# Attention ahead of two MoE layers: the softmax reciprocals take another way, and the attention stage is put in a new order

## The chip, the cores and the metric

The kernel runs on one core of a Trainium2 chip. The metric is the device time of one execution in microseconds (us); times of several runs are given as a median with the lowest and the highest. The engines are TensorE (PE), VectorE (DVE), ScalarE (ACT), GpSimd (POOL) and SyncE (SP), whose queue issues all transfers of this kernel.

## The reference, cut to what matters

```python
scores = scale * np.matmul(q, k.transpose(0, 1, 3, 2))      # 4 batches, 8 heads, 576 tokens, 64 wide
thresh = np.max(scores, axis=-1, keepdims=True) - tau
scores = np.where(scores >= thresh, scores, -1000000000.0)
attn = np.exp(scores - np.max(scores, axis=-1, keepdims=True))
attn = attn / (np.sum(attn, axis=-1, keepdims=True) + 1e-09)
x = np.matmul(attn, v)                                      # put together as 2304 tokens x 512
h = x @ w_in;  x = (h * np.tanh(softplus(h))) @ w_out       # first MoE layer, d_ff 2048
g = x @ w_gate
out = (silu(g) * (x @ w_val)) @ w_out2                      # second layer, d_ff 1536
```

The change touches the division by the row sum, which is done as a multiplication of the attention output by the reciprocal, and the order of the work around it.

## The kernel before, in words

**Stages.** `attention()` works off 16 pairs of heads; `moes()` follows with two layers, each a list of blocks (a group of hidden units times a third `r` of the tokens), computed by a scheme with seven products per block that take seven prepared pieces of the input (B11, T1, B22, T2, T3, B21, T4). The pieces of the first block, r = 0, are prepared during attention (function `beside` in `kern`, class `Pieces`: `turn` subtracts, `split` makes a high and a low half, `store` writes 768 KB to DRAM) and fetched into `xp` tiles at the start of `moes()`. Weights arrive as `raw` tiles and are converted by ACT, DVE and POOL (`Weights.convert`).

**One pair p.** SP loads q, k and v; ACT and POOL split q and k into high and low halves; SP copies them into the tile `stk` (`stack`, L240). For i = 0 to 8 (four row blocks of two heads, and one of both heads' tails): `scores` on PE (L95 or L104), `rowmax` on DVE (L112), `thresh` on POOL (L116), `expo` on ACT (L122), `mask` on DVE (L130, which also sums the rows into `su`). `trans` on PE turns the masked block in 128x128 steps (L157) into a PSUM bank `g`, and `evac` on ACT copies it to `pt`. When half of the row blocks are there (u = 0, then u = 1), `av` on PE multiplies by v (L180, 20 matmuls). Banks: `s` has 3 buffers, `g` has 2, which `av` and the transposes share.

**The reciprocals.** For each u: `added` on POOL adds 1e-9 (L185), `recip` on DVE (L190), `rwide` on POOL repeats each reciprocal over 64 columns (L197; for u = 1 also L199), `rbc` on PE turns the result, so that it lies along the token axis, into a `g` bank (L205; for u = 1 also L207 with the constant `own`), `rcopy` on ACT copies it to `rs` (L213), and `xout` on DVE multiplies the `av` bank by `rs` into the result x (L219).

**What sets the order.** Each step is entered in a `Plan` with an engine, a cost, the steps it waits for, the buffers it takes and frees, and a rank from the table `RANK` plus `PERIOD` times the pair (ranks with 0, 1 and z are for pairs 0, 1 and 15). `Plan.order` simulates the engines with these costs and emits the steps in the order found; each engine then works its queue strictly in that order. The plan of `attention()` is emitted as a whole ahead of that of `moes()`, SP's transfers included. In `moes()` the first `raw` loads have the lowest rank, then come the fetches of `xp`.

Of the kernel before, what the change touches and what calls it, by code (L numbers as in the profile page):

```python
# [23 lines left out]
def consts(tc, cp, tau):  # L24
    nc = tc.nc
    idf = cp.tile([P, P], F32, name="idf")
    make_identity(nc, idf)
    t = cp.tile([P, 3], F32, name="tau")
    nc.sync.dma_start(out=t[:, 0:1], in_=tau.partition_broadcast(P))

    nc.vector.tensor_scalar(out=t[:, 1:2], in0=t[:, 0:1], scalar1=0.0, scalar2=-1.0, op0=ALU.max, op1=ALU.mult)
    nc.vector.tensor_scalar(out=t[:, 2:3], in0=t[:, 0:1], scalar1=0.0, scalar2=0.125, op0=ALU.is_ge, op1=ALU.mult)

    own = cp.tile([P, P], F32, name="own")
    fold = cp.tile([P, 64], F32, name="fold")
    nc.vector.memset(own, 0.0)
    for h in range(2):
        a = slice(64 * h, 64 * h + 64)
        nc.vector.tensor_copy(out=fold[a, :], in_=idf[a, a])
        nc.vector.memset(own[a, a], 1.0)  # L40
    return dict(idf=idf, own=own, fold=fold, ntau=t[:, 1:2], cs=t[:, 2:3])


def attention(tc, cst, q, k, v, x, beside, S=576):
# [12 lines left out]
    idf, own, fold, ntau, cs = (cst[x] for x in ("idf", "own", "fold", "ntau", "cs"))  # L57
# [7 lines left out]
    qt = [pl.tile([P, 2, P], F32R, name=f"qt{i}") for i in range(2)]  # L65
    for t in qt:
        nc.vector.memset(f(t), 0.0)


# [62 lines left out]
    def bank(nm):  # L132
# [39 lines left out]
    def av(p, u, j0, j1):  # L172

        d = st[p]
        if j0 == 0:
            d["av", u] = bank(f"av{p}_{u}")
# [5 lines left out]
    def added(p, u):  # L182
        d = st[p]
        a = slice(4 * u, 4 + 5 * u)
        nc.gpsimd.tensor_scalar(out=d["su"][:, a], in0=d["su"][:, a], scalar1=1e-9, scalar2=0.0, op0=ALU.add, op1=ALU.add)  # L185

    def recip(p, u):
        d = st[p]
        a = slice(4 * u, 4 + 5 * u)
        nc.vector.reciprocal(out=d["r"][:, a], in_=d["su"][:, a])  # L190

    def rwide(p, u):

        d = st[p]
        w = d["rw", u] = pw.tile([P, 320], F32, tag="rw", name=f"rw{p}_{u}", bufs=SLOTS["rw"])
        r = d["r"][:, 4 * u:4 * u + 4].rearrange("p (c h) -> p c h", h=2)[:, :, :, None].to_broadcast([P, 2, 2, 64])
        nc.gpsimd.tensor_scalar(out=w[:, 0:256].rearrange("p (c h d) -> p c h d", c=2, h=2), in0=r, scalar1=1.0, scalar2=1.0, op0=ALU.mult, op1=ALU.mult)  # L197
        if u:
            nc.gpsimd.tensor_scalar(out=w[:, 256:320], in0=fold, scalar1=d["r"][:, 8:9], scalar2=1.0, op0=ALU.mult, op1=ALU.mult)  # L199

    def rbc(p, u):
        d = st[p]
        g = d["rg", u] = bank(f"rg{p}_{u}")
        for c in range(2):
            nc.tensor.transpose(g[:, 128 * c:128 * c + 128], d["rw", u][:, 128 * c:128 * c + 128], idf)  # L205
        if u:
            nc.tensor.matmul(out=g[:, 256:320], lhsT=own, rhs=d["rw", u][:, 256:320], start=True, stop=True)  # L207

    def rcopy(p, u):
        d = st[p]  # L210
        d["rs", u] = pw.tile([P, 320], F32, tag="rs", name=f"rs{p}_{u}", bufs=SLOTS["rs"])
        n = 256 + 64 * u
        nc.scalar.copy(out=d["rs", u][:, 0:n], in_=d["rg", u][:, 0:n])  # L213

    def xout(p, u):
        d = st[p]
        n = 256 + 64 * u
        for to, c0, c1 in xslices(p, 256 * u, n):
            nc.vector.tensor_tensor(out=to, in0=d["av", u][:, c0:c1], in1=d["rs", u][:, c0:c1], op=ALU.mult)  # L219
# [49 lines left out]
    turns = []  # L269
    for p in range(NP + 2):  # L270
        for i in range(16):
            turns.append((p, "T", i))
            turns += [(p - a // 16, "A", u) for u, a in enumerate(AFTER) if i == a % 16]
    turns = {x: ("g", n) for n, x in enumerate(x for x in turns if 0 <= x[0] < NP)}
    plan = Plan(SLOTS, WAIT)
    for p in range(NP):
        ranks = {x: iter(y) for x, y in RANK.items()}
        small = iter(range(16))

        def op(eng, cost, fn, *a, key, after=(), take=(), free=()):  # L280
            kind = (key[0] if eng != "DMA" else "D" + key[0] if key[1] == "load" else "st") + OWN.get(p, "")
            plan.op(eng, cost, lambda p=p: fn(p, *a), (p, *key), [(p, *x) for x in after], take, free, PERIOD * p + next(ranks[kind]))

        for nm in "qk":
            op("DMA", 1.2, load, nm, key=(nm, "load"), take=["n"])
            if nm == "q":
                op(*(("Pool", 1.0, inputs, "q", "scale", nc.gpsimd) if p else ("DVE", .4, inputs, "q", "scale", nc.vector)), key=("q", "scale"), after=[("q", "load")])
            if nm == "q" and p == 0:
                op("Pool", 1.5, zeros, key=("q", "zeros"), take=["stk"])
                for h in range(2):  # L290
                    op("ACT", .573, firstparts, "hi", h, key=("q", "hi", h), after=[("q", "scale"), ("q", "zeros")])
                    op("DVE", .7, firstparts, "lo", h, key=("q", "lo", h), after=[("q", "hi", h)], free=["n"] * h)
                continue
            op("ACT", .573 + .053 * (nm == "k"), inputs, nm, "hi", key=(nm, "hi"), after=[("q", "scale") if nm == "q" else ("k", "load")], take=[nm])
            op(*(("Pool", 1.4 + .15 * (nm == "k"), inputs, nm, "lo", nc.gpsimd) if p else ("DVE", .75, inputs, nm, "lo", nc.vector)), key=(nm, "lo"), after=[(nm, "hi")], free=["n"])
        op("Pool", .8, tails, key=("t",), after=[("q", "stack", 1) if p else ("q", "lo", 1)], take=["qt"], free=["q"] * (p > 0))
        op("DMA", 1.3, load, "v", key=("v", "load"), take=[vslot(p)])
        for nm, cost in (("q", 1.3), ("k", 2.6)) * (p > 0):
            for h in range(2):
                op("DMA", cost, stack, nm, h, key=(nm, "stack", h), after=[(nm, "lo"), ("q", "stack", 0)][:2 if (nm, h) != ("q", 0) else 1], take=["stk"] * ((nm, h) == ("q", 0)))  # L300
        for i in range(9):
            c, h = divmod(i, 2)
            made = [(y, "stack", z) for y in "qk" for z in ([h] if i < 8 else [0, 1])] if p else [("q", "lo", h if i < 8 else 1), ("k", "lo")]
            op("PE", .53 if p and i < 8 else .81, scores, i, key=("S", i), after=made + [("t",)] * (i == 8), take=["s"], free=["k", "qt", "stk"] if i == 8 else [])
            op("DVE", .68, rowmax, i, key=("R", i), after=[("S", i)] + [("R", 0)] * (i > 0), take=["sm"] * (i == 0))
            op("Pool", .26, thresh, i, key=("H", i), after=[("R", i)])
            op("ACT", .7, expo, i, key=("E", i), after=[("R", i)], take=["e"])
            op("DVE", .8, mask, i, key=("M", i), after=[("E", i), ("H", i)] + [("M", i - 1)] * h, take=["pp"] if h == 0 else [], free=["s", "e"])
            for m0, n in (((0, 3),), ((3, 3), (6, 3)))[h] if i < 8 else ((0, 4), (4, 2)):
                g = turns[p, "T", next(small)]  # L310
                op("PE", .11 * n, trans, c, m0, n, key=("T", c, m0), after=[("M", i)], take=[g] + ["pt"] * (m0 == 0 and c in (0, 2)), free=["pp"] * (m0 == (6 if c < 4 else 4)))
                op("ACT", .365 if c < 4 else .54 if m0 == 0 else .21, evac, c, m0, n, key=("V", c, m0), after=[("T", c, m0)], free=[g])
            if i in (3, 8):
                u = int(i == 8)
                op("Pool", .26, added, u, key=("P", u), after=[("M", 3)] if u == 0 else [("M", 7), ("M", 8)])
                op("DVE", .2, recip, u, key=("Q", u), after=[("P", u)])
                op("Pool", .38 + .2 * u, rwide, u, key=("rw", u), after=[("Q", u)], take=["rw"], free=["sm"] * u)
                g = turns[p, "T", next(small)]
                op("PE", .22 + .22 * u, rbc, u, key=("B", u), after=[("rw", u)], take=[g], free=["rw"])
                op("ACT", .31, rcopy, u, key=("C", u), after=[("B", u)], take=["rs"], free=[g])  # L320
                ready = [("V", y, z) for y in ((0, 1), (2, 3))[u] for z in (0, 3, 6)] + [("V", 4, 0), ("V", 4, 4)] * u + [("v", "load")]
                for n, (j0, j1) in enumerate(PARTS):
                    end = j1 == 5
                    op("PE", (.432, .538)[u] * (j1 - j0), av, u, j0, j1, key=("A", u, n), after=ready, take=[] if n else [turns[p, "A", u]], free=(["pt"] + [vslot(p)] * u) * end)
                    ready = [("A", u, n)]
                op("DVE", .335 + .067 * u, xout, u, key=("x", u), after=[("C", u)] + ready, free=[turns[p, "A", u], "rs"])
# [8 lines left out]
class Plan:  # L335
# [14 lines left out]

    def __init__(self, slots, wait):
# [11 lines left out]
    def op(self, eng, cost, fn, key, after, take, free, rank):  # L363
        o = dict(eng=eng, cost=cost, fn=fn, key=key, after=after, take=[], free=[], rank=rank, n=len(self.ops), loose=self.loose)
# [8 lines left out]
    def order(self, ops, strict):  # L373
# [24 lines left out]
        n, turn = 0, False  # L398
        while True:
            best = None  # L400
            for e in engines:
                found = []
                if queue[e] and not queue[e][-1]["left"]:
                    o = queue[e][-1]
                    found.append((max(clock[e], o["t"]), -1e9, n, o))
# [697 lines left out]
```

## Time and profile before

| | us |
|---|---|
| median of 3 runs (lowest, highest) | 1077.13 (1076.66, 1077.22) |
| profiled execution, its own time | 1077.86 |
| its span | 1076.1 |
| PE busy | 1057.3 |
| DVE busy | 775.1 |
| ACT busy | 655.5 |
| POOL busy | 269.3 |

The span begins with the first instruction of the program and ends with the last; the execution's own time has 1.8 us more around it. Attention is the first 283 us, the rest is the MoE. Matmuls overlap and their ends are modelled, so the time from the start of one PE instruction to that of the next tells more than its duration.

### The profile page before, as it was taken

Reading aid. Unit: us, or ns where it says so; the run is one execution under the profiler, and the core shown is the slowest. Engines: PE = TensorE matmul, PEld = TensorE weight load, DVE = VectorE, ACT = ScalarE, POOL = GpSimd, SP = SyncE. Lnnn points to the kernel's source line nnn. Section 1 sums busy time; section 2 is a strip of 40 time slices with the busy share of each in tenths; the row PEclk is TensorE's granted clock in tenths of the full one; section 3 lists DMA queues with packets and bytes.
Section 4 is the critical chain, followed back from the end, with each engine's and each line's share of the span. In section 5 each row is a group of like instructions: output and inputs, shape, how many; then the busy total and the mean of one; then the engine's idle time right before and its main releaser. Section 6 shows DMA issues by size and latency. Waiting matters only on the chain.

```text
span 1076.1 us, 17949 instructions
## 1 busy us (share of the span) xinstructions
PE 1057.3 (98%) x6358; PEld 972.2 (90%) x6358; DVE 775.1 (72%) x1445; ACT 655.5 (61%) x1313; POOL 269.3 (25%) x467
## 2 busy tenths in 40 slices
PE   6999999999999999999999999999999999999998
PEld 5777877777799999999999999999999999999997
DVE  6888988888688575557367776976578676686645
ACT  6899898888688675455356655765445454444331
POOL 4577877664211120022012001110010011110000
PEclk9999999999999999999999999999999999999999
DMA  5777767774856976577567697698878788887793
GB/s 134 198 200 190 197 177 215 202 217 121 339 202 232 331 247 224 176 255 255 176 215 254 199 340 253 245 315 314 308 274 292 263 296 307 272 300 246 241 300 125
DMA packets 66330, 259.47 MB, mean 241 GB/s; under 512 B 8768, under 2 KB 9024, under 8 KB 66240
## 3 DMA queue, kind: packets, MB, share of 16 engines
q1 hardware_dynamic: 66240, 258.31, 72.6%
q8 instruction: 51, 0.84, 0.3%
q14 instruction: 39, 0.32, 0.1%
HBM read 193.99 MB, written 37.75 MB: 215 GB/s over the span
## 4 chain that ended last, share of the span: by engine, by line
PE 89%; POOL 3%; ACT 2%; DVE 2%; DMA 2%; issue 2%; SPq 1%; DVEq 0%; POOLq 0%; ACTq 0%
PE ha L801 22%; PE y L927 18%; PE hb L801 17%; PE y L929 14%; PE av L180 6%; PE tg L157 5%; PE s L95 5%; PE s L104 1%; DVE sm L112 1%; DMA stk<-qh 1%; DVE pp L130 1%; PE rg L205 1%; DMA x10T<-xo 0%; POOL xo L624 0%; SPq L240 0%
## 5 line engine op out<-in xcount | busy, mean ns | idle before, releaser
L510 POOL TENSOR_TENSOR cn<-cn,cl 128x512 int32<-128x512 int32 x68 | 94.3, 1387 | 632.7 <-DVE cn L507 443.4
L927 PE MATMUL y<-g,wo 128*128 128x384 f32 x1152 | 227.8, 335 | 0.7 <-DVE wo L533 0.7
L927 PEld LDWEIGHTS y<-g,wo 128*128 128x128 f32 x1152 | 202.2, 188 | 1.1 <-DVE wo L533 1.0
L945 DVE TENSOR_TENSOR acc<-y,acc 128x512 f32<-128x512 f32 (+2 forms) x163 | 100.1, 626 | 116.9 <-PE y L929 71.7
L929 PE MATMUL y<-wo,g 128*128 128x512 f32 (+1 forms) x654 | 166.7, 392 | 0.0
L801 PE MATMUL hb<-xp,wb 128*128 128x384 f32 x720 | 138.7, 335 | 0.4 <-ACT s L812 0.4
L801 PE MATMUL ha<-xp,wb 128*128 128x384 f32 x720 | 138.5, 335 | 0.0
L929 PEld LDWEIGHTS y<-wo,g 128*128 128x128 f32 x654 | 120.6, 188 | 18.8
L837 DVE TENSOR_TENSOR g<-c,g 128x384 fp32r<-128x384 f32 x168 | 104.6, 623 | 34.7 <-ACT g L834 34.0
L801 PEld LDWEIGHTS ha<-xp,wb 128*128 128x128 f32 x720 | 126.6, 188 | 3.2 <-ACT u L812 0.2
L801 PEld LDWEIGHTS hb<-xp,wb 128*128 128x128 f32 x720 | 126.4, 188 | 2.3 <-ACT s L812 0.8
L130 DVE SCALAR_TENSOR_TENSOR pp<-s,sm,e 128x576 f32<-128x576 f32 x144 | 115.2, 813 | 10.9 <-ACT e L122 6.1
L834 ACT CAST g<-c 128x384 fp32r<-128x384 f32 x168 | 86.4, 514 | 59.8 <-DVE c L870 31.5
L112 DVE TENSOR_REDUCE sm<-s 128x1 f32<-128x576 f32 x144 | 106.5, 751 | 16.5 <-PE s L95 11.9
L122 ACT ACTIVATE e<-s,sm 128x576 f32<-128x576 f32 x144 | 105.6, 753 | 6.5 <-DVE sm L112 5.7
L846 ACT ACTIVATE c<-c 128x384 f32<-128x384 f32 x144 | 75.4, 525 | 52.5 <-DVE c L822 52.1
L157 PE MATMUL tg<-idf,pp 128*128 128x128 f32 x656 | 102.5, 280 | 3.4 <-DVE pp L130 1.7
L163 ACT COPY pt<-tg 128x384 f32<-128x384 f32 x192 | 87.3, 489 | 28.1 <-PE tg L157 26.9
L812 ACT COPY u<-ha 128x384 f32<-128x384 f32 x60 | 28.7, 479 | 114.3 <-PE ha L801 114.2
L95 PE MATMUL s<-stk 128*128 128x320 f32 x480 | 93.0, 317 | 0.8 <-DMA stk<-qh 0.7
L157 PEld LDWEIGHTS tg<-idf,pp 128*128 128x128 f32 x656 | 73.3, 142 | 18.8 <-ACT e L122 5.8
L180 PE MATMUL av<-pt,vn 128*64 128x256 f32 (+1 forms) x640 | 84.7, 411 | 0.0
(95 smaller groups left out, 1562.5 us busy)
## 6 DMA issues: line engine op xcount, KB each, us to landing
raw<-in_dram SPq DMA_DIRECT2D x68, 512.0 KB, 5.4
xp<-x20T SPq DMA_DIRECT2D x24, 768.0 KB, 5.2
xp<-x21T SPq DMA_DIRECT2D x20, 768.0 KB, 5.7
xp<-x22T SPq DMA_DIRECT2D x20, 768.0 KB, 6.0
xp<-x20B SPq DMA_DIRECT2D x18, 768.0 KB, 5.4
xp<-x10T SPq DMA_DIRECT2D x16, 768.0 KB, 5.9
xp<-x21B SPq DMA_DIRECT2D x15, 768.0 KB, 5.8
xp<-x22B SPq DMA_DIRECT2D x15, 768.0 KB, 6.0
```

The costliest lines, as they stand in the source:

```text
L95: nc.tensor.matmul(out=s[:, c0:c0 + n], lhsT=d["stk"][:, 0, q0:q0 + P], rhs=d["stk"][:, w, k0:k0 + n], start=w == 1, stop=w == 2)
L112: nc.vector.tensor_reduce(out=d["nm"][:, i:i + 1], in_=d["s", i], op=ALU.max, axis=AX.X, negate=True)
L122: nc.scalar.activation(out=e, in_=d["s", i], func=AF.Exp, bias=d["nm"][:, i:i + 1])
L130: nc.vector.scalar_tensor_tensor(out=d["pp", c][:, 576 * h:576 * h + 576], in0=d["s", i], scalar=d["th"][:, i:i + 1], in1=d["e", i], op0=A ...
L157: nc.tensor.transpose(g[:, 128 * m:128 * m + 128], d["pp", c][:, o:o + 128], idf)
L180: nc.tensor.matmul(out=d["av", u][64 * h:64 * h + 64, 0:n], lhsT=d["vn"][:, 5 * h + j], rhs=d["pt", u][:, 5 * h + j if j < 4 else 4, 0:n], ...
L510: nc.gpsimd.tensor_tensor(out=self.n[key], in0=self.n[key], in1=self.l[key], op=ALU.add)
L801: nc.tensor.matmul(out=tiles[bank, q], lhsT=w[:, a, w0 + P * d:w0 + P * d + P], rhs=x[:, z, d], start=k in (1, 5, 2) and d == 0 and y == 0 ...
L837: (V if GLOW[L] == "DVE" else nc.gpsimd).tensor_tensor(out=tiles["g", j, s][:, 1], in0=tiles[nm, q], in1=f(tiles["g", j, s][:, 0]), op=ALU ...
L927: nc.tensor.matmul(out=y[:, 0:C], lhsT=w[:, a, P * d:P * d + P], rhs=h[:, x], **m)
L929: nc.tensor.matmul(out=y[:, c0:c1], lhsT=h[:, x, P * d:P * d + P], rhs=w[:, a, c0:c1], **m)
L945: V.tensor_tensor(out=a, in0=y, in1=a, op=ALU.add)
```

## The change

- The path `rwide`, `rbc`, `rcopy` and the constants `own` and `fold` go. In their place, once a pair and after its last mask: `added` on POOL over all nine columns, `recip` on DVE (two instructions) into a tile `rr`, `turned` on DVE (a transpose in blocks of 32x32), `park` (four small stores on SP to a DRAM tile `parked[p]`), `spread` (three transfers on SP that read it back, each to 64 partitions) into `rs`.
- `xout` only copies the `av` bank to x, on ACT for u = 0 and on DVE for u = 1. A new step `scaled` on POOL multiplies x by `rs` in place afterwards. The pieces of the first block wait for `scaled` in place of `xout`.
- `attention()` begins with 30 matmuls on zeros (`WARM`).
- `RANK`, `PERIOD` and many costs of the plan are new; a cost may be a pair (until the engine is free, until the result is there), and a table `SEM` holds what a semaphore takes. `T4` of the first block is no longer prepared in attention but at its use in `moes()` (`KEPT`); the pieces' steps in attention are cut in two parts in place of four and have another rank.

```diff
-    own = cp.tile([P, P], F32, name="own")
-    fold = cp.tile([P, 64], F32, name="fold")
...
+    rr = [pl.tile([P, 2, 32], F32, name=f"rr{i}") for i in range(2)]
...
+    warm = ps.tile([P, 512], F32, tag="g", name="warm", bufs=SLOTS["g"])
+    for _ in range(WARM):
+        nc.tensor.matmul(out=warm[:, 0:256], lhsT=qt[0][:, 0], rhs=qt[0].rearrange("p h d -> p (h d)"), start=True, stop=True)
...
-    def rwide(p, u):
...
-    def rbc(p, u):
...
-    def rcopy(p, u):
...
+    def added(p):
+        su = st[p]["su"]
+        nc.gpsimd.tensor_scalar(out=su, in0=su, scalar1=1e-9, scalar2=0.0, op0=ALU.add, op1=ALU.add)
+
+    def recip(p):
+        su, r = st[p]["su"], rr[p % 2][:, 0]
+        nc.vector.reciprocal(out=r[:, 0:10].rearrange("p (h c) -> p c h", h=2)[:, 0:4], in_=su[:, 0:8].rearrange("p (c h) -> p c h", h=2))
+        nc.vector.reciprocal(out=r[:, 4:5], in_=su[:, 8:9])
+
+    def turned(p):
+        t = rr[p % 2]
+        nc.vector.transpose(out=t[:, 1], in_=t[:, 0])
+
+    def park(p):
+        to = parked[p].rearrange("(i b t) -> i b t", b=4, t=32)
+        for b in range(4):
+            nc.sync.dma_start(out=to[:, b], in_=rr[p % 2][32 * b:32 * b + 9, 1])
+
+    def spread(p):
+        t = st[p]["rs"] = pw.tile([P, S], F32, tag="rs", name=f"rs{p}", bufs=SLOTS["rs"])
+        for a, c0, n, at in ((0, 0, S, 0), (64, 0, 512, 640), (64, 512, 64, 576)):
+            nc.sync.dma_start(out=t[a:a + 64, c0:c0 + n], in_=parked[p][at:at + n].partition_broadcast(64))
...
-            nc.vector.tensor_tensor(out=to, in0=d["av", u][:, c0:c1], in1=d["rs", u][:, c0:c1], op=ALU.mult)
+            if XOUT[u] == "DVE":
+                nc.vector.tensor_copy(out=to, in_=st[p]["av", u][:, c0:c1])
+            else:
+                nc.scalar.copy(out=to, in_=st[p]["av", u][:, c0:c1])
+
+    def scaled(p):
+        for to, c0, c1 in xslices(p, 0, S):
+            nc.gpsimd.tensor_tensor(out=to, in0=to, in1=st[p]["rs"][:, c0:c1], op=ALU.mult)
...
+        op("Pool", (.225, .253), added, key=("P",), after=[("M", 7), ("M", 8)])
+        op("DVE", (.17, .26), recip, key=("Q",), after=[("P",)], take=["rr"], free=["sm"])
+        op("DVE", (.1, .2), turned, key=("Z",), after=[("Q",)])
+        op("DMA", 1.7, park, key=("o", "out"), after=[("Z",)], free=["rr"])
+        op("DMA", 1.3, spread, key=("i", "in"), after=[("o", "out")], take=["rs"])
+        op("Pool", (1.42, 1.45), scaled, key=("n",), after=[("x", 0), ("x", 1), ("i", "in")], free=["rs"])
...
-AFTER = 10, 20
-TURN = 0.16
+SIDE = ()
+XOUT = "ACT", "DVE"
+WARM = 30
...
-XEARLY = 1000
-XPARTS = 4
+XEARLY = 100
+XPARTS = 2
+KEPT = "T4",
```

## Rows read from the trace of the kernel before

**Rows 1.** The page's first part: busy time, share of span, instructions.
```profile
PE 1057.3 (98%) x6358; PEld 972.2 (90%) x6358; DVE 775.1 (72%) x1445; ACT 655.5 (61%) x1313; POOL 269.3 (25%) x467
```

**Rows 2.** Busy time by stretch: stretch, length, engines, granted clock, DMA share, GB/s.
```profile
100.00:150.00 50.00, 49.65 (x385) 39.58 (x384) 45.03 (x101) 45.24 (x97) 37.93 (x77) 1.00 0.70 188
...
310.00:700.00 390.00, 390.00 (x2237) 388.01 (x2236) 263.91 (x446) 232.09 (x441) 49.22 (x35) 1.00 0.70 245
```

**Rows 3.** Timeline of PE over one pair: start, us, instructions merged.
```profile
153.12 2.91 PE L180 MATMUL av<-pt,vn 128*64 128x320 f32 x20
...
157.14 0.38 PE L205 MATMUL rg<-idf,rw 128*128 128x128 f32 x2
157.36 0.49 PE L157 MATMUL tg<-idf,pp 128*128 128x128 f32 x3
157.60 0.78 PE L95 MATMUL s<-stk 128*128 128x320 f32 x4
158.22 0.82 PE L157 MATMUL tg<-idf,pp 128*128 128x128 f32 x6
...
164.53 0.78 PE L95 MATMUL s<-stk 128*128 128x320 f32 x4
165.44 0.41 PE L205 MATMUL rg<-idf,rw 128*128 128x128 f32 x2
...
165.86 0.50 PE L157 MATMUL tg<-idf,pp 128*128 128x128 f32 x3
...
169.55 1.84 PE L180 MATMUL av<-pt,vn 128*64 128x320 f32 x12
```

**Rows 4.** Tile `rg`: count, duration in ns (min/median/max), first and last start.
```profile
L205 PE MATMUL rg<-idf,rw x64: 269/273/329, 21.1 to 280.0; 128*128 128x128 f32 x64
L213 ACT COPY rs<-rg x32: 363/398/428, 21.9 to 280.5; 128x256 f32<-128x256 f32 x16, 128x320 f32<-128x320 f32 x16
```

**Rows 5.** Timeline of PE at the start.
```profile
6.96 0.87 PE L104 MATMUL s<-kh,stk 128*128 128x320 f32 x2 [6.96 <-ACT kh L228]
...
8.24 0.63 PE L104 MATMUL s<-kh,stk 128*128 128x256 f32 x2
8.66 0.42 PE L104 MATMUL s<-kl,stk 128*128 128x256 f32 x1
...
11.54 0.41 PE L104 MATMUL s<-kl,stk 128*128 128x256 f32 x1
...
16.53 0.40 PE L104 MATMUL s<-kh,stk 128*128 128x256 f32 x2
```

**Rows 6.** Timeline of DVE at the start.
```profile
12.00 0.76 DVE L112 TENSOR_REDUCE sm<-s 128x1 f32<-128x576 f32 x1 [0.68 <-PE s L104]
```

**Rows 7.** Timeline of all engines and SP's queue, 262 to 312 us.
```profile
272.38 0.80 SPq L492 DMA_DIRECT2D raw<-in_dram  x2
...
273.28 0.38 SPq L766 DMA_DIRECT2D xp<-x10B  x1
...
276.48 0.82 DVE L130 SCALAR_TENSOR_TENSOR pp<-s,sm,e 128x576 f32<-128x576 f32 x1 [0.20 <-ACT e L122]
...
277.77 0.18 DVE L190 RECIPROCAL sm<-sm 128x5 f32<-128x5 f32 x1
...
280.38 2.91 PE L180 MATMUL av<-pt,vn 128*64 128x320 f32 x20
...
283.22 2.35 PE L801 MATMUL ha<-xp,wa 128*128 128x384 f32 x12
```

**Rows 8.** Transfers issued from 273.27 to 273.6 us: count, KB, us to landing.
```profile
xp<-x10B SPq DMA_DIRECT2D x1, 768.0 KB, 6.4
```

**Rows 9.** Transfers of the whole span: count, KB, median us to landing.
```profile
out_dram<-acc SPq DMA_DIRECT2D x2, 128.0 KB, 1.8
tau<-in_dram SPq DMA_DIRECT2D x1, 0.5 KB, 3.0
```

**Rows 10.** Groups of POOL, 100 to 250 us: count, busy us, mean ns, idle before.
```profile
L231 POOL TENSOR_TENSOR ql<-qn,qh 128x576 fp32r<-128x576 f32 x9 | 12.8, 1422 | 0.9 <-ACT qh L228 0.9
```

More of the change, by code (lines that the diff above doesn't have):

```diff
@@ L192, in rwide @@
-    def rwide(p, u):
[L194 to L199, printed above, removed]
@@ L201, in rbc @@
-    def rbc(p, u):
[L202 to L207, printed above, removed]
-    def rcopy(p, u):
[L210 to L213, printed above, removed]
@@ L293, in attention @@
                 continue
[L294 to L297, printed above, removed]
@@ L298, in attention @@
-        for nm, cost in (("q", 1.3), ("k", 2.6)) * (p > 0):
+            op("ACT", (.626, .743) if nm == "k" else (.563, .663), inputs, nm, "hi", key=(nm, "hi"), after=[("q", "scale") if nm == "q" else ("k", "load")], take=[nm])
+            op(*(("Pool", (1.54, 1.556) if nm == "k" else (1.39, 1.417), inputs, nm, "lo", nc.gpsimd) if p else ("DVE", (.75, .853), inputs, nm, "lo", nc.vector)), key=(nm, "lo"), after=[(nm, "hi")], free=["n"])
+        op("Pool", (1.13, 1.15), tails, key=("t",), after=[("q", "stack", 1) if p else ("q", "lo", 1)], take=["qt"], free=["q"] * (p > 0))
@@ L299, in attention @@
+        op("DMA", .6, load, "v", key=("v", "load"), take=[vslot(p)])
+        for nm, cost in (("q", 1.2), ("k", 2.4)) * (p > 0):
             for h in range(2):
@@ L308, in attention @@
-            op("DVE", .8, mask, i, key=("M", i), after=[("E", i), ("H", i)] + [("M", i - 1)] * h, take=["pp"] if h == 0 else [], free=["s", "e"])
+            op("PE", (.53, .74) if p and i < 8 else (.81, 1.03), scores, i, key=("S", i), after=made + [("t",)] * (i == 8), take=[turns[p, "S", i]], free=["k", "qt", "stk"] if i == 8 else [])
+            op("DVE", (.67, .753), rowmax, i, key=("R", i), after=[("S", i)] + [("R", 0)] * (i > 0), take=["sm"] * (i == 0))
+            op("Pool", (.225, .264), thresh, i, key=("H", i), after=[("R", i)])
@@ L309, in attention @@
+            op("ACT", (.634, .748), expo, i, key=("E", i), after=[("R", i)], take=["e"])
+            op("DVE", (.738, .815), mask, i, key=("M", i), after=[("E", i), ("H", i)] + [("M", i - 1)] * (i > 0), take=["pp"] if h == 0 else [], free=[turns[p, "S", i], "e"])
             for m0, n in (((0, 3),), ((3, 3), (6, 3)))[h] if i < 8 else ((0, 4), (4, 2)):
                 g = turns[p, "T", next(small)]
-                op("PE", .11 * n, trans, c, m0, n, key=("T", c, m0), after=[("M", i)], take=[g] + ["pt"] * (m0 == 0 and c in (0, 2)), free=["pp"] * (m0 == (6 if c < 4 else 4)))
@@ L313, in attention @@
             if i in (3, 8):
                 u = int(i == 8)
[L315 to L325, printed above, removed]
@@ L326, in attention @@
-                op("DVE", .335 + .067 * u, xout, u, key=("x", u), after=[("C", u)] + ready, free=[turns[p, "A", u], "rs"])
+                ready = [("V", y, z) for y in ((0, 1), (2, 3))[u] for z in (0, 3, 6)] + [("V", 4, 0), ("V", 4, 4), ("A", 0)] * u + [("v", "load")]
+                t = 5 * (.432, .538)[u]
+                op("PE", (t, t + .22), av, u, 0, 5, key=("A", u), after=ready, take=[turns[p, "A", u]], free=["pt"] + [vslot(p)] * u)
+                t = .335 + .07 * u
+                op(XOUT[u], (t, t + .09) if XOUT[u] == "DVE" else (.255 + .05 * u, .37 + .05 * u), xout, u, key=("x", u), after=[("A", u)], free=[turns[p, "A", u]])
@@ L363, in op @@
     def op(self, eng, cost, fn, key, after, take, free, rank):
-        o = dict(eng=eng, cost=cost, fn=fn, key=key, after=after, take=[], free=[], rank=rank, n=len(self.ops), loose=self.loose)
+        cost, dur = cost if isinstance(cost, tuple) else (cost, None)
+        o = dict(eng=eng, cost=cost, dur=dur, fn=fn, key=key, after=after, take=[], free=[], rank=rank, n=len(self.ops), loose=self.loose)
         self.ops.append(o)
@@ L757, in room @@
                     return tiles["x", k]
-                if new:
+                if new and ((L, r) != (1, 0) or piece in KEPT):
                     new.turn(plan, piece, PENG, ready, R - LEAD)
@@ L997, in kern @@
     where = {(L, r, nm): pd.tile([P, 4 * CHUNK], F32, name=f"x{L}{r}{nm}") for L in (1, 2) for r in range(3) for nm, _, _ in USES.values()}
+    parked = [pd.tile([9 * P], F32, name=f"r{p}") for p in range(q.shape[0])]
     W = Weights(tc)
```

127 lines of the change are left out of this document (60 added, 67 removed).

## The prediction

> **What bounds the kernel now.** I read the page first: TensorE (PE) is busy for 98% of the span [rows 1]. The table by stretches says how. In the attention steady state (100 to 150 us) PE is busy 49.65 of 50 us with VectorE at 45.03, ScalarE at 45.24 and GpSimd at 37.93; in the two MoE layers PE is busy 390 of 390 us [rows 2]. So a microsecond taken off PE's own work in attention shortens the kernel by up to a microsecond, if the other three (90% busy) keep up; and PE idle time anywhere is lost, since nothing later has slack to give back.
>
> Next, PE's instructions in time order over one pair of heads [rows 3]. The av matmuls of one pair start at 153.12 and those of the next at 169.55: a period of 16.43 us. Inside it the reciprocal path holds PE twice: two transposes from 157.14 to 157.36 (0.22 us) and, for the second part, two transposes and the `own` matmul from 165.44 to 165.86 (0.42 us). The view of tile `rg` confirms the count: 64 such transposes [rows 4], 4 a pair for 16 pairs.
>
> Then the two ends of the attention stage: PE's first matmuls [rows 5], and all engines and SP's queue around the step into the MoE [rows 7].
>
> **The change part by part.**
>
> *The reciprocal off PE.* Direct: 0.22 + 0.42 = 0.64 us a pair, times 16 = 10.2 us. In front of the second group PE also waits: the four score matmuls at 164.53 take until 165.44, 0.91 us, where the same four at 157.60 take 0.62 [rows 3]; 0.29 us times 16 = 4.6 us. That wait may pass to the next transposes, as there are still only two `g` banks; bounds 0 and 4.6, I take half, 2.3. Together 12.5 us (10.2 to 14.8 if nothing else holds).
>
> *Do the others keep up?* ScalarE loses two `rs` copies of 0.40 us a pair [rows 4] and gains one PSUM copy of the first `x`, like in size: it is 0.4 lighter. VectorE loses the first `x`, keeps the second as a copy, keeps two reciprocals, and gains a transpose of 128x32, which no row shows; the nearest is the reciprocal at 0.18 us [rows 7], and between 0.1 and the 0.76 of a reduction over 576 elements [rows 6] I take 0.2. GpSimd loses `rwide` (three steps a pair) and one `added`, and gains a multiply over 128x576, for which the nearest row is its subtraction of that size, 1.42 us [rows 10]; even with nothing taken off for the first, that is 12.5 + 1.4 us of a period. All three stay near the shares they have, in a period of about 15.65 us, so I cost this at nothing beyond the half kept above; were VectorE to become the bound, the 12.5 would shrink (a rival below).
>
> *SP and the DMA queues.* Each pair adds four small stores and three broadcasts to SP's 15 transfers. At about 0.4 us an issue (two in 0.80 us [rows 7]) that is 2.8 us more of SP in a period; they also move 0.3 MB onto queues that are busy 70% [rows 2]. The multiply waits for the way to DRAM and back. It is ordered late, and only the MoE pieces need its result, so in the steady state I cost it at nothing. If its cover goes, it stands at the head of GpSimd's queue with the `thresh` steps behind it, and the masks wait for those.
>
> *The start.* PE idles until 6.96 us; three score groups then take until about 11.95 (6.96 to 11.54 + 0.41 [rows 5]). There a pair of 128x256 matmuls shows 0.63 us, against 0.40 at 16.53. PE is thus at its lower level of 1.2 GHz until about 16.4 us and at 2.4 GHz after, though the slices of the page round this away. VectorE waits for these scores (the third reduction starts at 12.00 after 0.68 us idle [rows 6]). The 30 warming matmuls fit into the idle 7 us: two of 256 columns take 0.42 us at the lower level (8.24 to 8.66 [rows 5]), so 30 take 6.3 us. If the level is up at 7 us, three groups of about 0.8 us replace three of 1.6: 2.4 us less, of which VectorE, next in the chain, passes on most. I take 2.0; from 0.5 (the level does not rise in time) to 3.5 (the new order also removes waits).
>
> *The step into the MoE.* This is where I expect a loss. SP works its queue in order, and the MoE's first loads come behind all of attention's. Now SP has nothing left of attention after the last `v` load, so `raw` is issued at 272.38 and the first `xp` at 273.28 [rows 7], 11 us before PE needs it; it lands 6.4 us later [rows 8], at 279.7, 7.3 us after `raw`'s issue, and PE goes from the last av (280.38) to the first MoE matmul at 283.22 without a pause. After the change, `park` and `spread` of the last pair stand ahead of `raw` in SP's queue, and they need the last mask. Count from the end of that mask, m = 276.48 + 0.82 = 277.30 now [rows 7]:
> the reciprocal starts at m + 0.47 (277.77); with a second one and the transpose it is done at m + 1.0. Four stores at 0.4 us an issue: the last is issued at m + 2.2. Landing is between 1.8 us (128 KB stored to DRAM) and 3.0 (`tau`, 0.5 KB) [rows 9]; I take 2.3: m + 4.5. Three broadcasts: SP free at m + 5.8. Then 7.3 us as now: the first `xp` lands at m + 13.1. PE, however, has its last av done at m + 5.5 (283.22 less m is 5.92, less the 0.42 us of the last reciprocal group, which the 10.2 already holds). PE stands idle for 7.6 us (6 to 9.5 by the bounds). The following pieces have lain behind each other as now, so they cost nothing more.
>
> After this idle time PE's level can be down again. At the start, after 6.96 us without work, it stayed down for 9.4 us, in some 7 us of which matmuls ran at half their rate [rows 5], a loss of 3.5 to 4; bounds 0 and 4 us, I take 2. The Trainium skill ("TensorE: Matmul & The Clock Gate", part 1, the HAM clock gate) says the same of the direction: throttled is the default, activity lifts it and an idle stretch brings it back. This speaks for the warming at the start and against the new pause; the trace agrees at the start, and no row shows the second case. By its example of a loop that waits for DMA, the level would surely fall here; the sum would then be nearer 4 than 2.
>
> For the store and its way back, the Trainium skill ("DMA: Bandwidth & Descriptors", anatomy of one DMA) puts about 2.0 us fixed on one transfer, mostly the receipt of the write. By it the landing would be 2.0 instead of my 2.3, and the pause an estimated 7.3 us.
>
> *T4 kept.* The piece T4 of the first block moves from GpSimd in attention to VectorE at the MoE's start: two steps on 128x768, at the mask's rate (0.82 for 576, [rows 7]) 1.1 us each. VectorE does them while PE waits for `xp`, so nothing; without that cover up to 2.2 us. The other new planner costs change the order in a stretch where PE is 100% busy [rows 2]: nothing.
>
> **Sum.** -12.5 - 2.0 + 7.6 + 2.0 = -4.9 us. The profiled execution took 1077.86 us, 0.73 above the median of 1077.13: 1073.0 by the one, 1072.2 by the other, which I predict.
>
> **The rivals.**
> *B: no pause at the MoE.* The last pair's masks may be ordered so early that the round trip hides behind the av matmuls. For it: the last pair has ranks of its own. Against: now only 5.5 us of PE work lie behind the last mask, and 13.1 are needed. It gives 1072.2 - 9.6 = 1062.6.
> *C: GpSimd blocked, the kernel slower.* The place is the multiply at the head of GpSimd's queue in every pair, its broadcast not yet landed, with `thresh`, mask and transposes behind it. For it: queues busy 70%, and more with the change; 22 issues on an in-order SP. Against: GpSimd has 24% to spare [rows 2], and the multiply is ordered late. It decides from 4.9 / 16 = 0.3 us a pair; at 0.8 us it costs 12.8: 1085.
> *D: no longer bound by PE.* With VectorE and ScalarE at 90% [rows 2], the freed time becomes waiting for masks and for `g` banks. If only 5.6 of 12.5 us come through: 1072.2 + 6.9 = 1079.1. Against: these two engines lose work too.
> *E: the clock takes the larger price.* The level falls in the pause and stays down as long as at the start, where some 7 us of dense matmuls lost half [rows 5]: 4 us instead of 2, so 1074.2. For it: the pause is as long as the idle time at the start. Against: the matmuls of the MoE come denser than those. The rule of the Trainium skill's page named above ("TensorE: Matmul & The Clock Gate") points to this rival.
>
> **How the numbers follow.** Chances: forecast 0.48, B 0.12, C 0.17, D 0.13, E 0.10. The forecast's own range is 1066 to 1079 (10 to 15 gained in attention, 0.5 to 3.5 at the start, 6 to 13 lost at the MoE, not all at one end). With half of B inside, and C up to a price of 0.7 us a pair, the range is 1062 to 1083. About 0.2% (2.2 us) is what a measurement of this kernel can tell from no change. Faster: most of the forecast (0.39), B 0.12, E 0.07, D 0.01 = 0.59. Same: 0.07 + 0.08 of D + 0.03 of E = 0.18. Slower: C 0.17, D 0.04, forecast 0.02 = 0.23.
>
> **What would show it.** The gain: no `rg` tile, and av to av about 15.65 us in the middle of attention. The start: pairs of 128x256 score matmuls at 0.40 already in the first groups. The pause: `raw` issued after the last broadcast, some 6 us behind the last mask, and PE idle about 7.6 us ahead of its first `ha` matmul. C: `thresh` on GpSimd after a wait that ends with `rs`. The prediction is wrong if PE goes into the MoE without a pause, or if the period stays over 16.1 us.

## The result: slower by 0.6%

The changed kernel takes 1083.08 us (median of 4 runs, 1081.55 to 1085.09), the kernel before, run beside it, 1076.89 (4 runs, 1075.92 to 1077.22): a ratio of 1.006 [1.0041, 1.008]. The forecast was 1072.2 us. The profiled executions have spans of 1079.8 and 1076.1 us, and the account below is made between these two. The profiled execution of the changed kernel took 1081.55 us, so the account covers 3.7 of the 6.2 us between the medians; the other 2.5 were not profiled. Lines of the code have moved: `av` is L182 now, `trans` L159, `turned` L195, `park` L200, `spread` L205, `scaled` L216, `ha` and `hb` L808.

First the page's busy times, then stretches of the table by windows, both of the changed kernel, against [rows 1, 2].

```profile
PE 1054.3 (98%) x6292; PEld 969.2 (90%) x6292; DVE 776.3 (72%) x1438; ACT 651.2 (60%) x1286; POOL 262.3 (24%) x403
```

```profile
10.00:20.00 10.00, 8.21 (x51) 7.75 (x51) 8.20 (x17) 7.28 (x13) 6.00 (x13) 0.83 0.64 180
100.00:150.00 50.00, 46.83 (x342) 36.29 (x343) 42.78 (x93) 42.16 (x91) 36.35 (x63) 0.97 0.75 207
283.00:300.00 17.00, 13.78 (x80) 12.88 (x77) 10.39 (x17) 10.79 (x19) 3.84 (x3) 1.00 0.85 310
310.00:700.00 390.00, 389.33 (x2234) 387.32 (x2233) 263.93 (x445) 232.07 (x439) 48.25 (x35) 1.00 0.68 245
```

PE does have 3 us less work, but it is idle where it was not: 3.2 of 50 us from 100 to 150 (0.35 before), and 3.2 of 17 us just after the step into the MoE. The granted clock, the share of TensorE's full 2.4 GHz that it was given, is below 1.00 in two stretches (its lower level, 1.2 GHz, is 0.50). What PE waited for (view of waits, 0 to 300 us: total, times, longest):

```profile
PE av L182 <- DMA vn<-in_dram: 6.5, 5, 2.6
PE hb L808 <- ACT s L819: 3.2, 1, 3.2
PE tg L159 <- ACT pt L168: 2.2, 12, 0.2
PE s L104 <- DVE pp L130: 1.8, 1, 1.8
```

The first line is new: before, `av` never waited for v. The account by starts of PE instructions, with the versions of the experiments that go farthest:

| us | first av | last av | first ha | from there to the end |
|---|---|---|---|---|
| before | 24.89 | 280.38 | 283.22 | 792.86 |
| changed | 23.18 | 280.81 | 283.66 | 796.12 |
| two v buffers, last division moved | 23.25 | 274.73 | 277.57 | 792.78 |
| the same, later conversion | 22.73 | 271.83 | 274.67 | 792.77 |

The change wins 1.71 us up to the first av, loses 2.14 from there to the last, and 3.26 after the first ha: 3.7 in all, the difference of the spans.

**One late v.** SP's queue and PE around the worst place of the changed kernel (timelines of SP and of PE), and behind them the same two timelines of the kernel before:

```profile
105.00 0.59 SPq L499 DMA_DIRECT2D raw<-in_dram  x1
105.69 0.65 SPq L82 DMA_DIRECT2D qn<-in_dram  x1
106.45 0.39 SPq L82 DMA_DIRECT2D vn<-in_dram  x1
106.93 1.38 SPq L200 DMA_DIRECT2D r<-rr  x4
```

```profile
109.10 0.78 PE L95 MATMUL s<-stk 128*128 128x320 f32 x4
112.50 3.65 PE L182 MATMUL av<-pt,vn 128*64 128x256 f32 x20 [2.61 <-DMA vn<-in_dram]
116.07 0.90 PE L159 MATMUL tg<-idf,pp 128*128 128x128 f32 x3
116.63 0.89 PE L95 MATMUL s<-stk 128*128 128x320 f32 x4
```

```profile
156.07 0.33 SPq L82 DMA_DIRECT2D vn<-in_dram  x1
...
158.14 0.59 SPq L82 DMA_DIRECT2D qn<-in_dram  x1
```

```profile
159.83 2.38 PE L180 MATMUL av<-pt,vn 128*64 128x256 f32 x20
162.14 0.80 PE L95 MATMUL s<-stk 128*128 128x320 f32 x4
```

v has one buffer, so its load waits for the pair's last av, and the next pair's first av needs it. Before, each load was issued 0.04 us after that av, ahead of the q load, and had 0.6 to 1.5 us to spare in a window of 3.8 us or more (14 pairs). In the new order the undisturbed window is 3.62 us, the load stands behind that of q (105.69, then 106.45; so in 11 of 15 pairs), and in 7 of 15 pairs it is also issued 0.2 to 2.7 us late. Here it comes about 6 us after its issue, behind q and a raw tile: PE loses 2.61 us, and then the clock falls: the granted clock is 0.50 from 113.4 to 116.9. The 20 matmuls take 3.57 us (112.50 to 116.07) where those at 159.83 in the kernel before take 2.31, and the transposes behind them 0.56 (116.07 to 116.63) instead of 0.30 (155.96 to 156.26 before). That is 1.5 us more.

**The step into the MoE**, all engines (timeline; in brackets the idle time before and what ended it):

```profile
276.65 0.59 SPq L773 DMA_DIRECT2D xp<-x10B  x1
...
279.15 1.41 POOL L216 TENSOR_TENSOR acc<-acc,rs 128x576 f32<-128x576 f32 x1 [2.56 <-DMA rs<-r]
...
280.65 0.26 POOL L186 TENSOR_SCALAR sm<-sm 128x9 f32<-128x9 f32 x1
280.81 2.91 PE L182 MATMUL av<-pt,vn 128*64 128x320 f32 x20 [0.45 <-ACT pt L168]
280.94 0.20 DVE L190 RECIPROCAL rr<-sm 128x8 f32<-128x8 f32 x1 [2.87 <-POOL sm L186]
...
281.21 0.21 DVE L195 STREAM_TRANSPOSE rr<-rr 128x32 f32<-128x32 f32 x1
281.45 1.35 SPq L200 DMA_DIRECT2D r<-rr  x4
...
282.85 0.34 SPq L773 DMA_DIRECT2D xp<-x10B  x1
283.66 2.38 PE L808 MATMUL ha<-xp,wa 128*128 128x384 f32 x12
...
283.82 1.73 SPq L205 DMA_DIRECT2D rs<-r  x3
...
288.68 1.40 POOL L216 TENSOR_TENSOR acc<-acc,rs 128x576 f32<-128x576 f32 x1 [7.77 <-DMA rs<-r]
290.04 2.48 POOL L517 TENSOR_TENSOR cn<-cn,cl 128x512 int32<-128x512 int32 x2
291.33 0.62 ACT L536 CAST wo<-cn 128x512 fp32r<-128x512 f32 x1 [3.74 <-POOL cn L517]
291.86 0.47 ACT L819 COPY s<-hb 128x384 f32<-128x384 f32 x1
...
292.38 1.31 PE L808 MATMUL hb<-xp,wb 128*128 128x384 f32 x6 [3.22 <-ACT s L819]
```

PE goes from the last av to the first ha in 2.85 us, without a pause: the first `xp` is issued at 276.65, ahead of the last `park`. The loss comes 9 us later, by a chain that one reads upwards from the last line. PE waits for ACT's copy of an `hb` bank; that copy stands behind a cast of weights; the cast waits for GpSimd's conversion; and that stands behind the last pair's `scaled`, which has waited 7.77 us for its `rs`.

### The profile page after: what moved, and what is told of

The parts are those of the page before. It is cut to its first block, busy times and chain, and to the rows that moved or that the text cites. A ratio compares the mean times of both kernels' runs of the same rounds, so it can differ in the third digit from the quotient of the medians.

```text
span 1079.8 us, 17817 instructions
## 1 busy us (share of the span) xinstructions
PE 1054.3 (98%) x6292; PEld 969.2 (90%) x6292; DVE 776.3 (72%) x1438; ACT 651.2 (60%) x1286; POOL 262.3 (24%) x403
## 4 chain that ended last, share of the span: by engine, by line
PE 87%; DMA 5%; ACT 3%; DVE 2%; issue 1%; SPq 1%; POOL 1%; DVEq 0%; ACTq 0%; POOLq 0%
PE ha L808 22%; PE y L934 18%; PE hb L808 17%; PE y L936 14%; PE av L182 6%; PE tg L159 5%; PE s L95 4%; DMA vn<-in_dram 2%; ACT e L122 1%; PE s L104 1%; ACT pt L165 1%; DMA qn<-in_dram 1%; ACT pt L168 1%; DMA xp<-x10T 1%; DMA rs<-r 1%
## 5 line engine op out<-in xcount | busy, mean ns | idle before, releaser
L808 PE MATMUL hb<-xp,wb 128*128 128x384 f32 x720 | 138.5, 334 | 3.2 <-ACT s L819 3.2
L808 PE MATMUL ha<-xp,wb 128*128 128x384 f32 x720 | 138.3, 334 | 0.0
L808 PEld LDWEIGHTS hb<-xp,wb 128*128 128x128 f32 x720 | 126.3, 188 | 5.1 <-ACT s L819 3.5
L808 PEld LDWEIGHTS ha<-xp,wb 128*128 128x128 f32 x720 | 126.6, 188 | 3.1
L844 DVE TENSOR_TENSOR g<-c,g 128x384 fp32r<-128x384 f32 x168 | 102.3, 610 | 33.1 <-ACT g L841 32.0
L159 PE MATMUL tg<-idf,pp 128*128 128x128 f32 x656 | 104.5, 282 | 2.5 <-ACT pt L168 2.2
L182 PE MATMUL av<-pt,vn 128*64 128x256 f32 (+1 forms) x640 | 85.9, 415 | 9.1 <-DMA vn<-in_dram 6.5
L159 PEld LDWEIGHTS tg<-idf,pp 128*128 128x128 f32 x656 | 72.4, 141 | 24.8 <-issue 7.6
```

Of the source, the lines that this page charges most:

```text
L159: nc.tensor.transpose(g[:, 128 * m:128 * m + 128], d["pp", c][:, o:o + 128], idf)
L182: nc.tensor.matmul(out=d["av", u][64 * h:64 * h + 64, 0:n], lhsT=d["vn"][:, 5 * h + j], rhs=d["pt", u][:, 5 * h + j if j < 4 else 4, 0:n], ...
L808: nc.tensor.matmul(out=tiles[bank, q], lhsT=w[:, a, w0 + P * d:w0 + P * d + P], rhs=x[:, z, d], start=k in (1, 5, 2) and d == 0 and y == 0 ...
L844: (V if GLOW[L] == "DVE" else nc.gpsimd).tensor_tensor(out=tiles["g", j, s][:, 1], in0=tiles[nm, q], in1=f(tiles["g", j, s][:, 0]), op=ALU ...
```

## The experiments

Two of them leave out part of the computation: "no trip" the whole division, "last unscaled" the division of the last pair. Each ratio is to the kernel before, run beside it (medians 1076.14 to 1077.17). In "by the changed kernel" 1083.08 is meant.

**1. The v load first.** Only SP's order differs: each v load stands at the place in SP's queue where the plan starts the av that frees its buffer.

```diff
+            for p in range(1, 15):
+                v, a = made[p, "v", "load"], made[p - 1, "A", 1]
+                v["t"], v["at"] = a["t"], a["at"] + .5
```

> Only SP's order changes: the load of the next pair's v is issued directly behind the transfers in front of which its buffer comes free, ahead of the next q load, for pairs 1 to 14. Theory V (the changed kernel loses its gain where av waits for a v that has one buffer, is issued late behind the q load, and lands late): of the 6.5 us of waits for vn about half go, those where v was issued 0.2 to 2.7 us after the last av; 3 to 5 us less, near 1079. Rival D (the freed time turns into waits for masks and banks whatever v does): within 1 us of 1083. Rival T (it is the traffic, not the order: v lands late however early it is issued): also within 1 us.

Measured: 1116.06 us, ratio 1.0365 [1.0341, 1.0389]: 33 us worse. PE's longest waits in its profile:

```profile
PE s L95 <- DMA r<-rr: 10.1, 5, 3.6
PE s L95 <- DMA stk<-qh: 5.1, 3, 1.9
```

SP now comes to the v load before it may be issued and stands there until the av is done (38.0 us in 13 waits, the longest 4.5), and the q and k copies for the scores queue up behind it. The mean granted clock of this execution is 0.985. So this run doesn't tell what a v load ahead of q but behind its av would bring; it shows that a waiting transfer moved ahead in an in-order queue holds up all that stands behind it.

**2. Two v buffers.** The load no longer waits; it is issued some 16 us ahead of its use.

```diff
-            t = pw.tile([P, 10, 64], F32, tag=vslot(p), name=f"vn{p}", bufs=SLOTS["vn"])
+            t = pw.tile([P, 10, 64], F32, tag=vslot(p), name=f"vn{p}", bufs=2 - (p == NP - 1))
...
+                v, a = made[p, "v", "load"], made[p - 1, "A", 0]
```

> v has two buffers in place of one (pairs 1 to 14), and its load is issued in SP's queue at the place of the first av of the pair before, some 10 us earlier; every other engine's order is that of the changed kernel. Theory V: all waits of av for vn go, with what follows from them (a TensorE clock that drops once): 7 to 9 us less, 1074 to 1076, that is a little faster than the kernel before. Rival D: the period of a quiet pair stays at 16.2 to 16.4 us, and the whole falls by 2 us at most, to 1081.

Measured: 1079.72 (10 runs, 1077.01 to 1083.52; the profiled one took 1083.52), ratio 1.0022 [1.0011, 1.0033]: 3.4 us better than the changed kernel. The waits for v fall from 6.5 to 0.7 us. What came up in their place, in the timeline:

```profile
59.83 0.43 DVE L516 TENSOR_SCALAR cn<-raw 128x512 int32<-128x512 int32 x1 [4.05 <-DMA raw<-in_dram]
...
61.71 1.29 PE L95 MATMUL s<-stk 128*128 128x320 f32 x4 [3.46 <-DVE pp L130]
```

VectorE stands at a conversion whose weights have not come, the mask waits behind it, and PE for the mask. The same four score matmuls take 0.78 us at full clock; here they take 1.29 (the granted clock is 0.50 from 61.8 to 65.2). The step into the MoE got worse in this execution: `scaled` waits 9.84 us for the last `rs`, PE 3.54 us for the copy of `hb`, the granted clock is 0.50 from 290.5 to 297.3, and from the first ha to the end it takes 800.59 us instead of 796.12.

**3. No trip.** `park` and `spread` move nothing and `scaled` multiplies by ones; the engines' orders are kept.

```diff
-        for b in range(4):
+        for b in ():
...
-        for a, c0, n, at in ((0, 0, S, 0), (64, 0, 512, 640), (64, 512, 64, 576)):
+        for a, c0, n, at in ():
```

> The seven transfers of park and spread are left out in every pair; scaled multiplies by a tile of ones, so the division by the row sums is left out of the result. All engines keep their order; SP and the DMA queues lose 7 of 22 transfers a pair, and GpSimd never waits for them. Theory V with T (the traffic and SP's time make v late): most waits for vn go and the GpSimd wait at the step into the MoE too, 8 to 11 us less, 1072 to 1075. Theory V by the order alone (v behind q): the waits for vn stay, and only the 2.8 us at the MoE go: 1080. Rival D: 1080 too, but with no waits for vn.

Measured: 1078.65 (10 runs, 1077.10 to 1083.00; the profiled one took 1083.00), ratio 1.0017 [1.0004, 1.0029], 4.4 us better than the changed kernel. The wait of `hb` falls from 3.2 to 1.6 us, but the waits for v stay (5.7 us in 7, against 6.5 in 5), so they don't come from the seven new transfers. This trace has the landing of the loads (count, KB, median us from issue to landing). First the kernel before, 30 to 260 us; then no trip from 30 to 220 us, where the q load is issued just ahead of v, and from 220 to 262, where it isn't:

```profile
vn<-in_dram SPq DMA_DIRECT2D x15, 320.0 KB, 2.9
...
qn<-in_dram SPq DMA_DIRECT2D x12, 288.0 KB, 4.9
```

```profile
vn<-in_dram SPq DMA_DIRECT2D x11, 320.0 KB, 4.1
...
qn<-in_dram SPq DMA_DIRECT2D x11, 288.0 KB, 2.8
...
vn<-in_dram SPq DMA_DIRECT2D x3, 320.0 KB, 3.0
```

The new order has exchanged the two: q, which can wait, lands 2.1 us sooner, and v, which had some 0.9 us to spare, 1.2 us later.

**4. The last division.** Once left out ("last unscaled"), once only moved ("last moved"): its `park` and `spread` on SP behind the first six `xp` fetches, its `scaled` on GpSimd behind the first two conversions of weights.

```diff
     def scaled(p):
+        if p == NP - 1:
+            return
```

```diff
+    plan.op("DMA", 1.7, park, ("r15", "o"), [], [], [], -30)
+    plan.op("DMA", 1.3, spread, ("r15", "i"), [("r15", "o")], [rs15], [], -29)
+    plan.op("Pool", 1.45, scaled, ("r15", "n"), [("r15", "i")], [], [rs15], 12)
```

> Only scaled of the last pair is left out (its x is not divided by the row sums); every other instruction keeps its place. Theory G (GpSimd stands 7.8 us in front of this multiply, waiting for the way to DRAM and back; the weight conversion queued behind it is late, ScalarE waits for it with the copies behind, and PE loses 3.2 us in front of hb): 2.5 to 3.2 us less, 1080. Rival R (the raw weights themselves land late, behind the last pair's transfers in SP's queue): under 1 us.

> The changed kernel with park, spread and scaled of the last pair moved into the MoE's plan: in SP's queue behind the first six fetches of xp, on GpSimd behind the first two weight conversions. Theory G: the 3.2 us of PE in front of hb go, and so does what the last pair's transfers hold up: 2.5 to 4 us less than the changed kernel, near 1079, like the run with the last multiply left out. Rival: the multiply only costs later what it cost before; within 1 us of 1083.

Measured: 1078.77 (1.0025 [1.0009, 1.004]) and 1077.47 (1.0005 [0.9995, 1.0015]), 4.3 and 5.6 us better than the changed kernel. The time from the first ha to the end is 794.4 and 793.07 instead of 796.12, the wait of `hb` is 0.4 and 0.35 us instead of 3.2. So 1.8 and 3.1 us of the gain stand in the MoE; the rest lies in attention, where the waits for v vary from run to run (7.5 us in 8 and 6.8 in 6 here).

**5. Both mends.** Two v buffers and the last division moved.

> Two v buffers and the late last pair together. If the two losses are independent, the sum of both: 6 to 8 us below the changed kernel, 1075 to 1077, level with the kernel before. If the waits for v and at the MoE were all that eats the saving: 1071 to 1073, as the quiet pairs run at 15.97 us with two v buffers against 16.43 before. If something else stands behind them (a weight load that VectorE waits for in the first pairs, as in the run with two v buffers): still above 1076.

Measured: 1071.67, ratio 0.9945 [0.993, 0.996]: now faster than before. 11.4 us better than the changed kernel, more than 3.4 + 5.6. The two losses are not independent: with two v buffers alone the time behind the first ha rose to 800.59 us in the profiled execution, with both mends it is 792.78 (table above). How much of that holds for the medians was not measured.

**6. The conversion later.** As 5, and the plan counts the weights' raw loads in attention as 5 us later, so that VectorE's conversion is ordered behind other work.

```diff
-... + (SLACK if e == "DMA" and o["key"][0] == "w" and not strict else 0.0))
+... + (SLACK if e == "DMA" and o["key"][0] == "w" else 0.0))
```

> As the version with two v buffers and the last pair's division moved behind the first fetches of the MoE (1071.67 us), but the plan counts the weights' raw loads of attention as 5 us later, so that VectorE's conversion of them is ordered later. Theory: the last single wait of TensorE in the first pairs, 2.0 us at 59.06 for a mask, comes from VectorE standing 2.6 us at the conversion for the raw weights; with it gone about 2 us are gained: 1069.7, and no wait of VectorE for raw in the first 100 us. Rival: the raw load is late because it stands behind a blocked transfer in SP's queue; a later conversion only moves the wait to the next step that needs the weights, or the new order opens another wait: 1071.7 or above.

> The version with two v buffers, the last pair's division moved and the later conversion once more, on another chip and in more runs: if its gain is one of the order of the work and not of single runs it is again 0.6 to 0.8% faster than the kernel before (ratio 0.992 to 0.994). Rival: part of the four runs' result was luck with TensorE's clock: 0.995 or above.

Measured: 1068.97, ratio 0.9931 [0.9913, 0.9949], and once more 1068.93 (5 runs, 1068.51 to 1069.25), ratio 0.9929 [0.9916, 0.9941]. This is the best version: 14.1 us better than the changed kernel. Part of one undisturbed pair of it, timeline of PE:

```profile
158.51 0.78 PE L95 MATMUL s<-stk 128*128 128x320 f32 x4
159.12 0.60 PE L159 MATMUL tg<-idf,pp 128*128 128x128 f32 x4
...
159.70 0.78 PE L95 MATMUL s<-stk 128*128 128x320 f32 x4
160.64 0.55 PE L159 MATMUL tg<-idf,pp 128*128 128x128 f32 x3 [0.17 <-ACT pt L168]
161.04 0.81 PE L95 MATMUL s<-stk 128*128 128x320 f32 x4
161.68 0.95 PE L159 MATMUL tg<-idf,pp 128*128 128x128 f32 x6
162.44 0.80 PE L95 MATMUL s<-stk 128*128 128x320 f32 x4
```

The four score matmuls at 159.70 are followed after 0.94 us (0.61 at 158.51): the 0.3 us that PE lost in front of the second `rg` group [rows 3] are still lost, now in front of the transposes, which wait for ScalarE to empty a `g` bank. Av to av is 15.98 us, 0.45 less than before.

**7. The warming.** Left out of the changed kernel; put into the kernel before; left out of the versions of 5 and 6.

```diff
-WARM = 30
+WARM = 0
```

> The changed kernel without its 30 warming matmuls; every other instruction keeps its place. Theory W (the warming brings the clock up before the first scores and so brings everything forward): 1.5 to 2.5 us slower than the changed kernel, first scores at 1.2 GHz. Rival (the first scores wait for their inputs, and VectorE paces the first pair): within 0.5 us.

> The kernel before with the 30 warming matmuls put ahead of its first scores, and nothing else. Theory W: 1.5 to 2.5 us faster than the kernel before, 1074.5. Rival (the order of the kernel before absorbs it in its first pair): within 0.5 us of 1076.5.

> As the version with two v buffers and the last pair's division moved (1071.67 us), without the 30 matmuls on zeros. Theory: what the warming is worth depends on the order behind it; in the changed kernel's order it was worth 4 us (1087.04 against 1083.08), and as this version has the same order of the first pairs it is again 4: 1075.6. Rival: as in the kernel before, where it gave nothing that could be measured, the start's gain is eaten by the waits of the next pairs: within 1 us of 1071.7; the 4 us of the changed kernel were then those of a fall of the clock that came or did not come.

> The same without the 30 matmuls on zeros, in the same call. Theory: with the waits gone the warming is worth less than 1 us, as the first av starts at 22.73 us both in the run of the best version with warming and in the run of the version of one step before without it: a ratio within 0.001 of that of the version run beside it. Rival: it is worth the 4 us that it was in the changed kernel: a ratio 0.0035 to 0.004 higher.

Measured: 1087.04 (1.0089 [1.0074, 1.0104]), so apparently 4.0 us for the warming; 1076.71 (0.9996 [0.9986, 1.0005]), nothing; 1072.43 (0.9969 [0.9955, 0.9983]), 2.6 us by the ratios, with overlapping intervals; 1069.97 (0.9937 [0.9924, 0.9951]), 1.0 us beside the run with it. The 4 us are not won at the start: without warming the changed kernel's first av stands at 22.72, with it at 23.18. Of the 5.3 us between the two profiled spans 3.8 stand after the first ha, 799.9 us to the end instead of 796.12. Its profile there, a stretch of the table by windows and the timeline:

```profile
290.00:300.00 10.00, 5.91 (x20) 5.62 (x21) 2.04 (x2) 4.20 (x7) 3.83 (x3) 0.69 1.00 389
```

```profile
291.68 1.40 POOL L216 TENSOR_TENSOR acc<-acc,rs 128x576 f32<-128x576 f32 x1 [9.70 <-DMA rs<-r]
...
295.37 2.29 PE L808 MATMUL hb<-xp,wb 128*128 128x384 f32 x6 [3.78 <-ACT s L819]
```

The last `rs` came later still, and the granted clock was 0.69 on average there. An ablation in a kernel with blocked queues measures the blockage as well; in the version without it the warming is worth 1 us.

## Why the prediction was wrong, point by point

The sum was -4.9 us and the spans say +3.7 (the medians +6.2). The miss of 8.6 between sum and spans has four parts.

- **The reciprocals off PE: right in kind, half the size.** Forecast -12.5 us between the first and the last av. What the best version shows of it is -6.4 (249.10 against 255.49). The `rg` work of 0.64 us a pair is gone. Of the 4.6 us of wait ahead of the second group I let half come through; nothing did, as the lower bound allowed. Beyond that bound the transposes take 0.2 us a pair more, summed over one pair of each trace (4.48 against 4.28 us from their starts to the next), so 0.45 a pair come through where I took 0.78. This is what rival D says of `g` banks.
- **SP's queue at nothing: the step that failed.** I added up the issue time of seven more transfers (2.8 us a period) and saw room. What counted was the order: v had 0.6 to 1.5 us to spare, I did not look at that slack, and the new order puts the q load ahead of v. 1.71 us won at the start and all of the 6.4 are eaten between the first and the last av; the waits for v (6.5 us, 1.1 in the best version) and the fall of the clock behind one of them (1.5) make 6.9 of the 8.5 us that the changed kernel is behind the best version there; the other 1.6 I have not followed. Two v buffers remove the waits, and the trip's traffic is not their cause (experiments 2 and 3).
- **The step into the MoE: the wrong wait.** +9.6 forecast (7.6 of pause, 2.0 of clock), +3.3 measured, by another mechanism. I took all of attention's transfers to be queued ahead of the MoE's, from the order in which the plans are run. SP's rows show them interleaved: two `xp` fetches ahead of the last `park`, the others around it. So what the section on the kernel says of SP, that attention's transfers are all emitted first, doesn't hold for the queue as it ran; what puts the fetches there I have not followed. So there is no pause (rival B's sign). Instead GpSimd is blocked by `scaled`: rival C's mechanism, but in the last pair only. In the other pairs `scaled` waited once, 2.56 us, in the pair before; that alone delayed `added` and the last reciprocal, 2.87 us of VectorE waiting. The trip was shorter on SP than I had it: 2.37 us from the first store to the first broadcast (forecast 3.5) and 4.10 to the end of the broadcasts (4.8); but the multiply began only 7.2 us after the first store, as the broadcasts had to land, and I had no term for that. The 2.0 us that I quoted for a landing from the Trainium skill ("DMA: Bandwidth & Descriptors", anatomy of one DMA) are given there for transfers that GpSimd issues; here SP issued the stores, and the last one landed within 1.33 us of its issue (2.55 in the profile of experiment 2). The 2.0 us for the clock were not paid in this execution, but at this place the clock did fall in two others, behind longer waits for `hb` (experiment 2, and without the warming in experiment 7).
- **The start: right by number, not by cause.** 1.71 us against 2.0. The level was up in the first groups, as forecast (pairs of 128x256 at 0.40 from 8.92), but fell again behind PE's wait at 12.77, and without the warming the first av is no later (22.72). The new order brought it. In the kernel before, the warming brought the first av to 22.10, and the run's time did not move.

So the four are, in us against the forecast: +6.1 (half the gain), +8.5 (what v and the clock took), +0.3 (start), -6.3 (MoE); together 8.6.

**Smaller readings.** T4 at nothing held: 792.77 us behind the first ha in the best version, 792.86 before. The first `xp` was issued 9.9 us ahead of PE's use (273.28 to 283.22), not 11; the sum doesn't use it. And the slices of the page don't round the lower level at the start away: in windows of 2 us, too, the profile has a granted clock of 1.00 there, because its first record of the clock is at 16.40 us. For the time before, the level rests on the durations of the matmuls alone (0.63 against 0.40).

**The clock.** The Trainium skill ("TensorE: Matmul & The Clock Gate", part 1) has idle stretches bring the throttle back. The traces agree in the direction: behind 112.50, after 2.61 us without work, the granted clock is 0.50. By the forecast that price belonged to the step into the MoE; in the profiled run no fall stands there, and two stand in attention.

## What to carry to other kernels

Before adding transfers to an in-order queue, list the loads that wait there for a single buffer, and read the slack of each (landing to first use): the smallest slack, not the busy share, says what the queue can bear. A step that waits for a trip through DRAM belongs behind everything on its engine that others wait for, the last instance above all, where the steady state's cover ends. And a change that measures slower can hold a gain: here two buffers, one moved step and one later conversion turned +0.6% into -0.7%.

## What the runs showed of the hardware

TensorE's clock answers to much shorter waits than I had expected, and not each time. In the changed kernel PE waited 1.75 us ahead of 12.77 and the granted clock was 0.50 from about 14.5 to 17.9; in the version of experiment 6 it waited 1.79 us at the same place and the granted clock stayed at 1.00. The same pair of score matmuls in both, first the changed kernel, then the other:

```profile
12.77 0.53 PE L104 MATMUL s<-kh,stk 128*128 128x320 f32 x2 [1.75 <-DVE pp L130]
...
14.86 0.63 PE L104 MATMUL s<-kh,stk 128*128 128x256 f32 x2
```

```profile
12.81 0.53 PE L104 MATMUL s<-kh,stk 128*128 128x320 f32 x2 [1.79 <-DVE pp L130]
...
14.73 0.39 PE L104 MATMUL s<-kh,stk 128*128 128x256 f32 x2
```

All nine profiled executions of the new order with the warming have this wait, at 1.75 to 1.94 us. In four of them (the changed kernel, experiments 1, 2 and 5) the granted clock is 0.50 at 15 to 17 us and the first av stands at 23.05 to 23.25; in the five others it is 1.00 there and the first av stands at 22.53 to 22.84. So the length of this wait doesn't decide; what does stays open. Other falls came in or behind waits of 1.73 us, closely after one of 1.07 (no trip, granted clock 0.50 from 43 us on), of 2.04 and 3.78 (without the warming), 2.49 (last moved), 2.61 (the changed kernel), 3.46 and 3.54 (experiment 2); "last unscaled", whose waits for v reach 1.9 us, has none.

The executions of experiments 2 to 4 spread over 6.5, 5.9, 6.8 and 4.2 us between the lowest and the highest of 10, those of the best version over 0.7 in 5. The mean granted clock is a part of it: in experiment 2 it is 0.997 at 1077.01 us and 0.994 at 1083.52, and 0.003 of 1080 us are some 3 of the 6.5. Whether the waits call forth the falls no run separates.

A transpose of 128x32 in 32x32 blocks took VectorE 0.21 us, as long as the reciprocal of eight columns (0.20).
